# Attention scores on small TensorE pieces with VectorE turns, and a new order of first loads and weight conversions

## The chip, the cores and the metric

The kernel runs on one core of a Trainium2 chip. The metric is the device time of one execution in microseconds (us); the time of a kernel is the median of its runs. In the profile, PE is TensorE's products, PEld its weight loads, DVE is VectorE, ACT ScalarE, POOL GpSimd, and SP the engine that issues most loads. POOL's spans are rough, and PE's ends are modelled.

## What is computed

A memory attention over 8 batches of 8 heads with 576 positions and 32 memory slots feeds a gated layer (512 to 1536 to 512) and an ELU layer (512 to 2048 to 512). The weights come as float64; q and k are scaled by 200.

```python
a = softmax(phi, axis=2)                       # over 576 positions
k_m = einsum('bhsm,bhsd->bhmd', a, k)
v_m = einsum('bhsm,bhsd->bhmd', a, v)
attn = softmax(q @ k_m.T / sqrt(64))           # over 32 slots
x = (attn @ v_m) rearranged to 4608 x 512
x = (silu(x @ w_gate) * (x @ w_val)) @ w_out   # the first layer
g = x @ w_in
out = where(g > 0, g, exp(min(g, 0)) - 1) @ w_out2
```

## The kernel before

Every weight goes through `load_w` (L86 to L112): SP loads 128x512 pairs of words, ScalarE scales the high word (L100), VectorE makes four passes (L101, L102, L104, L105), and then GpSimd adds the two parts (L111, for gate and value weights) or, for the others, ScalarE rounds to the high part (L107) and GpSimd makes the low part in two operations (L108, L109). This is called a conversion below. A product of the layers is three TensorE instructions of 288 columns: high by high, high by low, low by high.

Stage one runs eight loops, one for each batch `b`. Batch b + 2 goes through `front_tasks`: the exponents of phi (L216 to L223), their transposes `a_T` (L234), the products with k and v `kv_mm` (L247: 40 instructions of 128 rows, 32 columns of weights and 128 moving columns; the page shows two records for each fp32 instruction), the scaling by VectorE `kv_out` (L255) and the transposes `kv_T` (L263). Batch b + 1 goes through `back_tasks`: `score` (L282, with q as the weights, positions on the partitions, the 32 slots of two heads side by side), softmax over groups of 32 (L286 to L297), and the transposes back with the split into high and low parts, `attn_T` (L307 to L311). `vw_tasks` multiplies v_m into the gate and value weights (L139, eight instructions of 64 rows by 32 columns with 512 moving columns; L143 and L144 split the result into VW). Between these stand the loop's own products: for both halves of 288 positions and UA = 4 units, `gate1` (pg), `val1` (pv, then h at L183, hh at L162 and hl at L164), and the output product `down1` (pd) of the half before, which goes to DRAM. The function `tick` takes the next few pieces from the list `todo` after each product; `spread` says over how many ticks the list lasts. Conversions stand in the same list: the pairs 2 to 5 of gate and value weights, one pair (four conversions) in each of the loops 1 to 4, and `w_out` for the units 4 to 6 in loop 6 and 7 to 11 in loop 7. Loop 7 also makes the VW of pairs 2 and 3 for batch 0.

Stage two runs the units 4 to 11 of all batches, with the attention reloaded (`load2`) and part sums from DRAM; stage three is the second layer. Conversions of its weights (`more_w2`) stand in both.

The order of the instructions on each engine is fixed when the program is built, by a scheduler that follows its own model of times; it goes by the order of the code, except that `together` keeps a group of products in one piece and `issue_after` binds one instruction behind another. On the chip each engine goes through its own list in order. The loads of SP stand in one such list too; a load waits for its buffer (two for raw weights, `wr_p`; six each for kv and q).

## Time and profile before

| what | value |
|---|---|
| median of three runs | 1632.61 us (1631.53 to 1634.37) |
| the profiled execution | 1629.19 us, its span 1627.4 us |
| mean granted clock of TensorE | 0.982 |
| busy PE / PEld | 1577.3 us (97%) / 1358.8 us (83%) |
| busy DVE / ACT / POOL | 962.4 (59%) / 659.3 (41%) / 169.4 us (10%) |
| moved by DMA | 136.34 MB |

Stage one ends at 388.6 us. A busy share is a mean over stages that differ; the rows by stretches further below show one for each loop. PE is counted busy while any product is in flight, so 100% doesn't say that it streams at its peak.

### The profile page before, as it was taken

The page shows a single profiled execution, that of the slowest core. Times are in us where ns is not written, and L with a number is a line of the kernel's source. Part 1 is how long each engine was busy: PE and PEld are TensorE (multiplying, and loading weights), DVE is VectorE, ACT ScalarE, POOL GpSimd, SP SyncE. Part 2 cuts the span into 40 slices and gives each one's busy share as a digit, 9 for nine tenths or more (in the row PEclk, how much of TensorE's full clock was granted, in tenths as well). Part 3 has the DMA queues.
Part 4 walks back from the last instruction along what each step waited for, and adds up shares of the span by engine and source line. Part 5 has one row for each costly group of instructions (what it writes and reads, how often), then busy time and mean ns, then how long its engine had stood idle before and what let it go on. Part 6 is the DMA issues. An engine that isn't in the chain of part 4 may idle for free.

```text
span 1627.4 us, 24651 instructions
## 1 busy us (share of the span) xinstructions
PE 1577.3 (97%) x9968; PEld 1358.8 (83%) x9968; DVE 962.4 (59%) x1718; ACT 659.3 (41%) x1281; POOL 169.4 (10%) x135
## 2 busy tenths in 40 slices
PE   6699999999999999999999999999999999999998
PEld 4588888888999999999987788888888888888887
DVE  5778777665444544443799755555555555555554
ACT  3455444454333333333455443434343434343333
POOL 1211111132011010100244200000000000000000
PEclk7699999999999999999999999999999999999999
DMA  8877443243222322221242010101010101010000
GB/s 300 272 251 251 166 140 133 76 167 108 73 94 82 101 74 83 85 87 45 87 149 91 34 33 0 52 1 52 1 52 1 52 0 53 1 52 0 26 1 26
DMA packets 65906, 136.34 MB, mean 84 GB/s; under 512 B 6912, under 2 KB 38656, under 8 KB 63744
## 3 DMA queue, kind: packets, MB, share of 16 engines
...
q14 instruction: 36, 0.29, 0.1%
...
## 4 chain that ended last, share of the span: by engine, by line
PE 80%; DVE 9%; DMA 7%; ACT 2%; issue 1%; SPq 0%; ACTq 0%; DVEq 0%
PE pu L534 7%; PE pu L535 7%; PE pu L533 7%; PE acc L559 7%; PE acc L560 7%; PE acc L561 7%; PE acc L156 4%; PE acc L158 4%; PE acc L157 4%; PE pg L151 3%; PE pv L151 3%; PE pvw L139 3%; PE pg L153 3%; PE pg L152 3%; PE pv L152 2%; PE pv L153 2%
## 5 line engine op out<-in xcount | busy, mean ns | idle before, releaser
L561 PE MATMUL acc<-whi,hl 128*128 128x512 f32 x576 | 222.5, 391 | 2.8 <-DVE hl L164 2.8
L559 PE MATMUL acc<-whi,hh 128*128 128x512 f32 x576 | 224.3, 389 | 0.1
L560 PE MATMUL acc<-wlo,hh 128*128 128x512 f32 x576 | 224.1, 389 | 0.0
L533 PE MATMUL pu<-x1s,whi 128*128 128x512 f32 x576 | 224.1, 389 | 0.0
L534 PE MATMUL pu<-x1s,whi 128*128 128x512 f32 x576 | 224.1, 389 | 0.0
L535 PE MATMUL pu<-x1s,wlo 128*128 128x512 f32 x576 | 224.1, 389 | 0.0
L548 DVE SCALAR_TENSOR_TENSOR g<-e,g 128x512 f32<-128x512 f32 x144 | 103.7, 720 | 159.2 <-ACT g L547 159.2
L162 ACT ACTIVATE hh<-g 128x512 fp32r<-128x512 f32 x144 | 91.0, 632 | 212.8 <-DVE g L549 209.4
L183 DVE SCALAR_TENSOR_TENSOR h<-s,pv 128x288 f32<-128x288 f32 x192 | 86.5, 450 | 146.5 <-PE pv L153 132.5
L546 ACT ACTIVATE e<-g 128x512 f32<-128x512 f32 x144 | 90.8, 631 | 202.8 <-DVE g L545 202.8
L164 DVE TENSOR_TENSOR hl<-g,hh 128x512 fp32r<-128x512 f32 x144 | 101.1, 702 | 88.5 <-ACT hh L162 88.4
L156 PE MATMUL acc<-hh,whi 128*128 128x288 f32 x512 | 151.3, 296 | 0.1
L157 PE MATMUL acc<-hh,wlo 128*128 128x288 f32 x512 | 150.5, 294 | 0.0
L158 PE MATMUL acc<-hl,whi 128*128 128x288 f32 x512 | 149.5, 295 | 0.0
L162 ACT ACTIVATE hh<-h 128x288 fp32r<-128x288 f32 x192 | 85.0, 443 | 153.1 <-DVE h L183 152.6
L164 DVE TENSOR_TENSOR hl<-h,hh 128x288 fp32r<-128x288 f32 x192 | 94.5, 492 | 65.0 <-ACT hh L162 65.0
L561 PEld LDWEIGHTS acc<-whi,hl 128*128 128x128 f32 x576 | 108.0, 188 | 28.5 <-DVE hl L164 6.2
L559 PEld LDWEIGHTS acc<-whi,hh 128*128 128x128 f32 x576 | 108.2, 188 | 22.7 <-ACT hh L162 0.5
L534 PEld LDWEIGHTS pu<-x1s,whi 128*128 128x128 f32 x576 | 108.3, 188 | 22.4
L560 PEld LDWEIGHTS acc<-wlo,hh 128*128 128x128 f32 x576 | 108.0, 188 | 22.4
L533 PEld LDWEIGHTS pu<-x1s,whi 128*128 128x128 f32 x576 | 108.1, 188 | 22.3
L535 PEld LDWEIGHTS pu<-x1s,wlo 128*128 128x128 f32 x576 | 108.1, 188 | 22.3
...
## 6 DMA issues: line engine op xcount, KB each, us to landing
...
```

The lines of the kernel that those rows point to most:

```text
L156: mm(ps, lhsT=w[0][:, ms], rhs=hs[0], start=start, stop=False)
L157: mm(ps, lhsT=w[1][:, ms], rhs=hs[0], start=False, stop=False)
L158: mm(ps, lhsT=w[0][:, ms], rhs=hs[1], start=False, stop=stop)
L162: act(out=hh, in_=h, func=AF.Copy)
L164: tt(out=hl, in0=h, in1=hh.bitcast(F32), op=ALU.subtract)
L533: mm(ps, lhsT=wh[:, k, :], rhs=xh, start=k == 0, stop=False)
L534: mm(ps, lhsT=wh[:, k, :], rhs=xl, start=False, stop=False)
L535: mm(ps, lhsT=wl[:, k, :], rhs=xh, start=False, stop=k == KD - 1)
L548: stt(out=g, in0=e, scalar=1.0, in1=g, op0=ALU.add, op1=ALU.mult)
L559: mm(accs[c], lhsT=hs[0][:, cs], rhs=wh, start=u == 0, stop=False)
L560: mm(accs[c], lhsT=hs[0][:, cs], rhs=wl_, start=False, stop=False)
L561: mm(accs[c], lhsT=hs[1][:, cs], rhs=wh, start=False, stop=u == NU2 - 1)
```

## The change

The scores are computed by slot: kT holds the 64x32 pieces of a head as weights, and 288 positions of q move through them. Eight such instructions (L280 of the new kernel) lie side by side on TensorE and fill two PSUM tiles of 128x288, with the slots of four heads on the partitions. VectorE turns each tile in blocks of 32x32 out of PSUM (L285), so that the 32 slots lie along a row; the softmax runs over one tile of 128x576 for each half; a third turn from SBUF to SBUF (L305) brings it back, and ScalarE (L307) and VectorE (L308) split it. The 20 score products and 10 transposes back of a batch, and GpSimd's zeros in kT, go. q comes in two loads instead of five. The last 64 positions of k and v lie on 128 partitions (64 for each group of heads), so `a_T` has nine transposes instead of ten; `kv_mm` runs the columns outside and the two groups inside.

The first loads come in the order phi and kv of batch 0, gate and value weights of pair 0, q of batch 0, pair 1, then phi and kv of batch 1; `front_tasks(1)` and the first four `w_out` conversions move into loop 0, with a spread of 18. The pairs 2 and 3 are converted over the loops 1 to 4, two conversions in each, and the pairs 4 and 5 in loop 7. There are four buffers for raw weights; other pools change their counts, so that 19 conversions of the second layer stand ahead of stage three instead of 20. The old bodies of `score`, `norm` and `attn_T` are above and left out here.

```diff
-NWA = 32
+NWA = 24
 NWB = 16
-NWE = 8
-NWC = 8
-NKV = 6
-NQ = 6
+NWE = 14
+NWC = 10
+NKV = 5
+NQ = 3
...
-    wr_p = ctx.enter_context(tc.tile_pool(name="wr", bufs=2))
+    wr_p = ctx.enter_context(tc.tile_pool(name="wr", bufs=4))
...
         def load_kv(self, c):
-            n = chunk(c)
-            t = self.kvr[c] = fr_p.tile([128, 2, 512], F32, tag="kvr", name="kvr", bufs=NKV)
-            nc.sync.dma_start(out=t[:n], in_=kv[self.b, 128 * c:128 * c + n])
-        def load_q(self, c):
-            n = chunk(c)
-            t = self.qr[c] = bk_p.tile([128, 512], F32, tag="qr", name="qr", bufs=NQ)
-            nc.sync.dma_start(out=t[:, :4 * n], in_=qT[self.b, :, 512 * c:512 * c + 4 * n])
+            t = self.kvr[c] = fr_p.tile([128, 1024 if c < 4 else 512], F32, tag="kvr" if c < 4 else "kv4",
+                                        name="kvr", bufs=NKV if c < 4 else 2)
+            nc.sync.dma_start(out=t, in_=kv[self.b, 128 * c:128 * c + 128] if c < 4 else kv4[self.b])
+        def load_q(self, hf):
+            t = self.qr[hf] = bk_p.tile([128, 4, HS], F32, tag="qr", name="qr", bufs=NQ)
+            nc.sync.dma_start(out=t, in_=qT[self.b, hf].rearrange("p (j s) -> p j s", j=4))
...
         def a_T(self, c0):
             if c0 == 0:
...
+                self.a = fr_p.tile([128, 9, 128], F32, tag="a", name="a")
+            ps = ps_fr.tile([128, 4, 128], F32, tag="at", name="ps_aT")
+            ph = self.ph.rearrange("p g s -> p (g s)")
+            if c0 == 4:
+                nc.tensor.transpose(out=ps[:, 0], in_=ph[:, 512:640], identity=ident)
+                act(out=self.a[:, 8], in_=ps[:, 0], func=AF.Copy)
+                return
+            for i in range(2):
                 for g in range(2):
...
+                    s0 = 128 * (c0 + i) + 640 * g
+                    nc.tensor.transpose(out=ps[:, 2 * i + g], in_=ph[:, s0:s0 + 128], identity=ident)
+            act(out=self.a[:, 2 * c0:2 * c0 + 4], in_=ps, func=AF.Copy)
...
             def head(c, g, j):
-                n = chunk(c)
-                t = self.kvr[c].rearrange("p t (j g d) -> p t g j d", j=4, g=2)
-                o = 128 * g + 32 * j
-                return mm(self.kvp[g][32 * j:32 * j + 32], lhsT=self.a[:n, c, o:o + 32], rhs=t[:n, :, g, j, :],
-                          start=start and c == cs[0], stop=stop and c == cs[-1])
-            together([lambda c=c, g=g, j=j: head(c, g, j) for c in cs for g in (1, 0) for j in range(4)])
+                col = slice(32 * j, 32 * j + 32)
+                if c < 4:
+                    a = self.a[:, 2 * c + g, col]
+                    t = self.kvr[c].rearrange("p (t j g d) -> p g j t d", t=2, j=4, g=2)[:, g, j]
+                else:
+                    r = slice(64 * g, 64 * g + 64)
+                    a, t = self.a[r, 8, col], self.kvr[c][r].rearrange("p (t j d) -> p j t d", t=2, j=4)[:, j]
+                return mm(self.kvp[g][col], lhsT=a, rhs=t, start=start and c == cs[0], stop=stop and c == cs[-1])
+            together([lambda c=c, g=g, j=j: head(c, g, j) for c in cs for j in range(4) for g in (1, 0)])
...
         def kv_T(self):
...
+            self.kT = bk_p.tile([128, 4, M], F32, tag="kT", name="kT", bufs=2)
+            act(out=self.kT, in_=ps[:, 0], func=AF.Copy)
...
-            self.kT = bk_p.tile([128, 4, 2, M], F32, tag="kT", name="kT", bufs=2)
+        def score(self, hf):
+            q = self.qr.pop(hf)
+            ps = [ps_at.tile([128, HS], F32, tag="at", name="ps_sc") for _ in range(2)]
+            def head(j, g):
+                r = slice(64 * g, 64 * g + 64)
+                return mm(ps[g][32 * j:32 * j + 32], lhsT=self.kT[r, j, :], rhs=q[r, j, :], start=True, stop=True)
+            together([lambda j=j, g=g: head(j, g) for j in range(4) for g in (1, 0)])
+            t = self.sc = bk_p.tile([128, 2, HS], F32, tag="sc", name="sc", bufs=2)
             for g in range(2):
-                r, o = slice(64 * g, 64 * g + 64), slice(64 - 64 * g, 128 - 64 * g)
-                nc.gpsimd.memset(self.kT[o, :, g, :], 0.0)
-                act(out=self.kT[r, :, g, :], in_=ps[r, 0], func=AF.Copy)
...
+                nc.vector.transpose(out=t[:, g], in_=ps[g])
+            sc = t.rearrange("p g (b m) -> p (g b) m", m=M)
+            mx = bk_p.tile([128, 2 * HS // M, 1], F32, tag="mx", name="mx", bufs=2)
+            nc.vector.tensor_reduce(out=mx, in_=sc, op=ALU.max, axis=AX.X)
+            tt(out=sc, in0=sc, in1=mx.to_broadcast([128, 2 * HS // M, M]), op=ALU.subtract)
             act(out=sc, in_=sc, func=AF.Exp, scale=1.0 / float(D) ** 0.5)
...
+        def norm(self, hf):
+            sc = self.sc.rearrange("p g (b m) -> p (g b) m", m=M)
+            sm = bk_p.tile([128, 2 * HS // M, 1], F32, tag="smx", name="smx", bufs=2)
             nc.vector.tensor_reduce(out=sm, in_=sc, op=ALU.add, axis=AX.X)
             nc.vector.tensor_scalar_add(out=sm, in0=sm, scalar1=1e-9)
             nc.vector.reciprocal(out=sm, in_=sm)
...
+            tt(out=sc, in0=sc, in1=sm.to_broadcast([128, 2 * HS // M, M]), op=ALU.mult)
+        def attn(self, hf):
+            if hf == 0:
                 self.at = av_p.tile([128, 2, 2, S], F32R, tag="at", name="at")
...
+            t = bk_p.tile([128, 2, HS], F32, tag="ex", name="ex")
+            nc.vector.transpose(out=t.rearrange("p g s -> p (g s)"), in_=self.sc.rearrange("p g s -> p (g s)"))
+            hi, lo = (self.at[:, i, :, HS * hf:HS * hf + HS] for i in range(2))
+            act(out=hi, in_=t, func=AF.Copy)
+            tt(out=lo, in0=t, in1=hi.bitcast(F32), op=ALU.subtract)
...
     def front_tasks(b):
-        z, nxt = Bs[b], Bs[b + 1] if b + 1 < B else None
+        z, nxt = Bs[b], Bs[b + 1] if 0 < b < B - 1 else None
...
     def back_tasks(b):
-        z, nxt = Bs[b], Bs[b + 1] if b + 1 < B else None
-        yield lambda: (z.score(0, 2), nxt and [nxt.load_q(c) for c in (0, 1)])
-        yield lambda: (z.score(2, 4), nxt and [nxt.load_q(c) for c in (2, 3)])
-        yield lambda: (z.score(4, 5), nxt and nxt.load_q(4), 0 < b < B - 2 and Bs[b + 2].phi())
-        yield lambda: z.norm(0, 2)
-        yield lambda: (z.attn_T(0, 2), setattr(z, 'mark1', z.mark))
-        yield lambda: (z.norm(2, 4), z.norm(4, 5))
-        yield lambda: (z.attn_T(2, 5), z.store_at())
+        z, nxt = Bs[b], Bs[b + 1] if 0 < b < B - 1 else None
+        yield lambda: z.score(0)
+        yield lambda: (z.norm(0), nxt and nxt.load_q(0))
+        yield lambda: (z.attn(0))
+        yield lambda: (z.score(1), 0 < b < B - 2 and Bs[b + 2].phi())
+        yield lambda: (z.norm(1), nxt and nxt.load_q(1))
+        yield lambda: (z.attn(1), z.store_at())
...
-    Bs[0].load_phi()
-    for c in range(NCH):
-        Bs[0].load_kv(c)
-    for c in range(NCH):
-        Bs[0].load_q(c)
+    def load(z):
+        z.load_phi()
+        for c in range(NCH):
+            z.load_kv(c)
+    def load_q(z):
+        for c in range(2):
+            z.load_q(c)
+    load(Bs[0])
     Bs[0].phi()
     run(front_tasks(0))
     for k in range(KD):
         load_wg(0, k, wa_p)
-    Bs[1].phi()
+    load_q(Bs[0])
     run(back_tasks(0))
     vw(0, 0, G2)
     for k in range(KD):
         load_wg(1, k, wa_p)
-    with ExitStack() as after:
-        for ins in Bs[0].mark1:
-            after.enter_context(tc.issue_after(ins.ins))
-        run(front_tasks(1))
-        Bs[2].phi()
+    load(Bs[1])
     vw(0, 1, G2)
-    for u in range(UA):
-        load_wo(u, wa_p)
...
+    def wg_tasks(p):
+        return [lambda k=k: load_wg(p, k, wa_p) for k in range(KD)]
...
+        if b == 0:
+            wo = [lambda u=u: load_wo(u, wa_p) for u in range(UA)]
+            f1 = [lambda: (Bs[1].phi(), load_q(Bs[1]))] + list(front_tasks(1)) + [lambda: Bs[2].phi()]
+            for i in range(max(len(wo), len(f1))):
+                todo += wo[i:i + 1] + f1[i:i + 1]
         if 1 <= b <= 4:
-            bk += [lambda k=k, p=b + 1: load_wg(p, k, wa_p) for k in range(KD)]
+            bk += [lambda k=k, p=2 + (b - 1) // 2: load_wg(p, k, wa_p) for k in (0, 1) if b % 2] + \
+                [lambda k=k, p=2 + (b - 1) // 2: load_wg(p, k, wa_p) for k in (2, 3) if b % 2 == 0]
...
-            fr += [lambda: load_wo(7, wb_p), lambda: vw(0, 2, V2), lambda: load_wo(8, wb_p),
-                   lambda: load_wo(9, wb_p), lambda: vw(0, 3, V2), lambda: load_wo(10, wb_p),
-                   lambda: load_wo(11, wb_p)]
+            fr += wg_tasks(4) + [lambda: load_wo(7, wb_p), lambda: vw(0, 2, V2), lambda: load_wo(8, wb_p)]
+            fr += wg_tasks(5) + [lambda: load_wo(9, wb_p), lambda: vw(0, 3, V2), lambda: load_wo(10, wb_p),
+                                 lambda: load_wo(11, wb_p)]
...
-        spread = 16 if b < B - 2 else 24
+        spread = 18 if b == 0 else 16 if b < B - 2 else 24
```

On TensorE, from the VW of pair 0 of batch 0 to the first gate product, before (ps_sc is a score, ps_atT a transpose back, ps_aT and ps_kvm the transposes of phi and the kv products, pvw a VW):

```order
L139 MATMUL pvw<-wg,vt 32x512 x8
L263 MATMUL ps_kvT<-ident,kvm 128x128 x2
L234 MATMUL ps_aT<-ident,ph 128x128 x4
L282 MATMUL ps_sc<-kT,qr 128x2x32 x11
L234 MATMUL ps_aT<-ident,ph 128x128 x4
L282 MATMUL ps_sc<-kT,qr 128x2x32 x5
L282 MATMUL ps_sc<-kT,qr 64x2x32 x4
L234 MATMUL ps_aT<-ident,ph 64x128 x2
L247 MATMUL ps_kvm<-kvr,a 32x128 x40
L307 MATMUL ps_atT<-ident,sc 128x128 x4
L139 MATMUL pvw<-wg,vt 32x512 x8
L151 MATMUL pg<-at,vw 128x288
```

and now:

```order
L139 MATMUL pvw<-wg,vt 32x512 x8
L235 MATMUL ps_aT<-ident,ph 128x128 x8
L229 MATMUL ps_aT<-ident,ph 128x128
L251 MATMUL ps_kvm<-kvr,a 32x128 x40
L265 MATMUL ps_kvT<-ident,kvm 128x128 x2
L280 MATMUL ps_sc<-qr,kT 32x288 x8
L235 MATMUL ps_aT<-ident,ph 128x128 x4
L139 MATMUL pvw<-wg,vt 32x512 x8
L151 MATMUL pg<-at,vw 128x288
```

Half of batch 1's scores and all its transposes back are gone from here; the VW of pair 0 stands ahead of batch 1's whole front.

On TensorE in loop 4, a score of the next batch before, between the loop's gate, value and VW products:

```order
L153 MATMUL pg<-at,vw 128x288
L282 MATMUL ps_sc<-kT,qr 128x2x32
L139 MATMUL pvw<-wg,vt 32x512 x4
L282 MATMUL ps_sc<-kT,qr 128x2x32
L282 MATMUL ps_sc<-kT,qr 64x2x32 x3
L139 MATMUL pvw<-wg,vt 32x512 x4
L282 MATMUL ps_sc<-kT,qr 64x2x32
L151 MATMUL pv<-at,vw 128x288
```

and now, between output and gate products:

```order
L157 MATMUL pd<-hh,wlo 128x288
L158 MATMUL pd<-hl,whi 128x288
L280 MATMUL ps_sc<-qr,kT 32x288 x8
L151 MATMUL pg<-at,vw 128x288
L152 MATMUL pg<-at,vw 128x288
```

The score stood in pieces between other products, and stands in one piece of eight.

On VectorE, the rows up to the first h of stage two, before:

```order
L105 SCALAR_TENSOR_TENSOR wc<-wr,wc 128x512
L183 SCALAR_TENSOR_TENSOR h<-s,pv 128x288
L164 TENSOR_TENSOR hl<-h,hh 128x288
L183 SCALAR_TENSOR_TENSOR h<-s,pv 128x288
L164 TENSOR_TENSOR hl<-h,hh 128x288
L144 TENSOR_TENSOR vw<-pvw,vw 128x512 x3
L183 SCALAR_TENSOR_TENSOR h<-s,pv 128x288
L164 TENSOR_TENSOR hl<-h,hh 128x288
```

and now:

```order
L105 SCALAR_TENSOR_TENSOR wc<-wr,wc 128x512
L101 TENSOR_SCALAR wc<-wv 128x512
L102 SCALAR_TENSOR_TENSOR wv<-wv,wc 128x512
L104 TENSOR_SCALAR wc<-wv 128x512
L105 SCALAR_TENSOR_TENSOR wc<-wr,wc 128x512
L144 TENSOR_TENSOR vw<-pvw,vw 128x512
L101 TENSOR_SCALAR wc<-wv 128x512
L102 SCALAR_TENSOR_TENSOR wv<-wv,wc 128x512
L144 TENSOR_TENSOR vw<-pvw,vw 128x512
L104 TENSOR_SCALAR wc<-wv 128x512
L144 TENSOR_TENSOR vw<-pvw,vw 128x512
L183 SCALAR_TENSOR_TENSOR h<-s,pv 128x288
```

The h and hl of loop 7 stood between the last conversion and stage two; now conversions stand there, up to the first h and behind it.

## Rows read from the trace of the kernel before

**Rows 1.** Busy time by stretches: stretch, length, then busy us (instructions) as headed.

```profile
0.00:67.30 67.30, 45.38 (x400) 34.08 (x400) 40.73 (x83) 23.22 (x49) 13.38 (x23) 0.67 0.86 299
67.30:116.70 49.40, 40.37 (x419) 34.60 (x412) 40.21 (x86) 26.90 (x66) 11.26 (x10) 0.90 0.72 238
116.70:161.00 44.30, 43.38 (x461) 38.22 (x459) 35.52 (x77) 23.76 (x59) 5.90 (x6) 1.00 0.76 251
161.00:201.50 40.50, 40.12 (x372) 35.12 (x369) 31.20 (x72) 20.10 (x49) 5.84 (x6) 1.00 0.53 179
201.50:241.70 40.20, 38.06 (x277) 32.46 (x276) 31.28 (x67) 17.86 (x42) 6.08 (x6) 0.96 0.42 141
241.70:280.90 39.20, 36.78 (x276) 31.64 (x275) 31.24 (x67) 17.56 (x40) 5.76 (x4) 1.00 0.41 138
280.90:317.00 36.10, 36.10 (x277) 31.68 (x276) 21.69 (x51) 15.11 (x36) 0.00 (x0) 1.00 0.18 67
317.00:348.80 31.80, 30.48 (x232) 26.91 (x231) 22.92 (x45) 15.84 (x37) 8.57 (x6) 1.00 0.43 146
348.80:388.60 39.80, 37.65 (x299) 32.93 (x297) 22.88 (x41) 21.11 (x46) 14.96 (x10) 1.00 0.49 173
```

Behind PE stand PEld, DVE, ACT and POOL, then PEclk, the DMA share and GB/s.

**Rows 2.** Page, section 4: shares of the chain that ended last.

```profile
PE 80%; DVE 9%; DMA 7%; ACT 2%; issue 1%; SPq 0%; ACTq 0%; DVEq 0%
```

**Rows 3.** Timeline of TensorE in loop 1: start, us, engine, line, operation, names, shapes.

```profile
123.28 1.00 PE L282 MATMUL ps_sc<-kT,qr 128*128 128x64 f32 x8
124.09 0.38 PE L156 MATMUL pd<-hh,whi 128*128 128x288 f32 x1
```

**Rows 4.** Timeline of TensorE in loop 3.

```profile
203.48 0.29 PE L152 MATMUL pv<-at,vw 128*128 128x288 f32 x1
203.61 0.29 PE L153 MATMUL pv<-at,vw 128*128 128x288 f32 x1
203.74 0.58 PE L307 MATMUL ps_atT<-ident,sc 128*128 128x128 f32 x3
204.25 0.40 PE L156 MATMUL pd<-hh,whi 128*128 128x288 f32 x1
```

**Rows 5.** Timeline of TensorE in stage two.

```profile
429.29 1.09 PE L139 MATMUL pvw<-wg,vt 64*32 64x512 f32 x16
430.31 0.40 PE L151 MATMUL pg<-at,vw 128*128 128x288 f32 x1
```

**Rows 6.** Timeline of TensorE in loop 0.

```profile
111.73 2.53 PE L247 MATMUL ps_kvm<-kvr,a 64*32 64x128 f32 x80
114.19 0.40 PE L151 MATMUL pv<-at,vw 128*128 128x288 f32 x1
```

**Rows 7.** VectorE by line and form, 100 to 350 us: busy, mean ns | idle before.

```profile
L183 DVE SCALAR_TENSOR_TENSOR h<-s,pv 128x288 f32<-128x288 f32 x51 | 22.8, 447 | 4.9 <-PE pv L153 2.5
...
L297 DVE TENSOR_TENSOR sc<-sc,smx 128x512 f32<-128x512 f32 x11 | 8.0, 726 | 0.0
...
L287 DVE TENSOR_TENSOR sc<-ps_sc,mx 128x512 f32<-128x512 f32 x10 | 6.8, 679 | 0.0
...
L216 DVE TENSOR_REDUCE nmx<-ph 128x2 f32<-128x1152 f32 x3 | 4.0, 1346 | 4.0 <-DMA ph<-phiT 4.0
```

**Rows 8.** Timeline of VectorE in loop 7.

```profile
356.76 0.42 DVE L101 TENSOR_SCALAR wc<-wv 128x512 int32<-128x512 int32 x1
...
357.83 0.45 DVE L164 TENSOR_TENSOR hl<-h,hh 128x288 fp32r<-128x288 f32 x1
...
359.26 0.45 DVE L183 SCALAR_TENSOR_TENSOR h<-s,pv 128x288 f32<-128x288 f32 x1
359.62 1.15 DVE L101 TENSOR_SCALAR wc<-wv 128x512 int32<-128x512 int32 x1
...
363.82 0.45 DVE L183 SCALAR_TENSOR_TENSOR h<-s,pv 128x288 f32<-128x288 f32 x1
```

**Rows 9.** Timeline of VectorE at the start; in brackets the idle time before.

```profile
15.37 0.61 DVE L255 TENSOR_SCALAR kvm<-ps_kvm,rs 128x128 f32<-128x128 f32 x2 [7.12 <-PE ps_kvm L247]
```

More of the change, by code (lines that the diff above doesn't have):

```diff
@@ L28, with attention_moe_moe @@
 NCH = 5
-NWA = 32
+NWA = 24
 NWB = 16
-NWE = 8
-NWC = 8
-NKV = 6
-NQ = 6
+NWE = 14
+NWC = 10
+NKV = 5
+NQ = 3
 @with_exitstack
-def attention_moe_moe(ctx: ExitStack, tc: tile.TileContext, qT, phiT, kv, w1g, w1o, w2, out):
+def attention_moe_moe(ctx: ExitStack, tc: tile.TileContext, qT, phiT, kv, kv4, w1g, w1o, w2, out):
     nc = tc.nc
@@ L226, in a_T @@
             if c0 == 0:
-                self.a = fr_p.tile([128, NCH, 256], F32, tag="a", name="a")
-            n = chunk(c0)
-            nch = 2 if n == 128 else 1
-            ps = ps_fr.tile([128, 2, 256], F32, tag="at", name="ps_aT")
-            for i in range(nch):
+                self.a = fr_p.tile([128, 9, 128], F32, tag="a", name="a")
[6 more added lines that the diff above has]
+            for i in range(2):
                 for g in range(2):
-                    s0 = 128 * (c0 + i)
-                    nc.tensor.transpose(out=ps[:n, i, 128 * g:128 * g + 128],
-                                        in_=self.ph[:, g, s0:s0 + n], identity=ident)
-            act(out=self.a[:n, c0:c0 + nch], in_=ps[:n, :nch], func=AF.Copy)
+                    s0 = 128 * (c0 + i) + 640 * g
+                    nc.tensor.transpose(out=ps[:, 2 * i + g], in_=ph[:, s0:s0 + 128], identity=ident)
+            act(out=self.a[:, 2 * c0:2 * c0 + 4], in_=ps, func=AF.Copy)
         def kv_mm(self, cs, start, stop):
@@ L512, in attention_moe_moe @@
                     nxt = load3(0)
-                if u % 2 == 1 if b == B - 1 else u == 8 and b < B - 2:
+                if u % 2 == 1 if b == B - 1 else u == 8 and len(w2q) > 8:
                     more_w2(w2q.pop(0))
@@ L593 @@
     gate, val = (inputs[n].reshape(KD, 128, NU1 // 2, 2, 1, 128) for n in ("moe_w_gate", "moe_w_val"))
+    ph = phi.reshape(B, 4, 2, S, M).transpose(0, 2, 1, 4, 3).reshape(B, 2, 128, S)
+    kvn = np.stack([a.transpose(0, 2, 1, 3).reshape(B, S, DM) for a in (k, v)], axis=2)
     arrays = {
[L595 to L597 removed]
+        "qT": qT.reshape(B, 128, 4, 2, HS).transpose(0, 3, 1, 2, 4).reshape(B, 2, 128, 4 * HS),
+        "phiT": np.stack([ph[:, 0], np.roll(ph[:, 1], 64, axis=2)], axis=1),
+        "kv": kvn[:, :512].reshape(B, 512, 1024),
+        "kv4": kvn[:, 512:].reshape(B, 64, 2, 4, 2, D).transpose(0, 4, 1, 2, 3, 5).reshape(B, 128, 512),
         "w1g": np.concatenate([gate, val], axis=4).transpose(2, 0, 1, 3, 4, 5).reshape(NU1 // 2, KD, 128, 512),
```

40 lines of the change are left out of this document (2 added, 38 removed).

## The prediction

> **What bounds the kernel now.** I read the busy time by stretches first, one for the start and one for each of the eight loops of stage one [rows 1], then the shares of the chain that ended last [rows 2]. The chain is 80% TensorE. In the stretches from 116.7 to 388.6 us TensorE is busy 94 to 100% of the time; only the first two, up to 116.7 (the start and loop 0), are otherwise: TensorE 45.4 of 67.3 and 40.4 of 49.4 us, at a granted clock of 0.67 and 0.90, beside DMA shares of 0.86 and 0.72 and VectorE at 40.7 and 40.2 us. The change touches stage one (loops 0 to 7) and the ends of the later stages, so the sum has three parts: A, from the start to the first gate product of batch 1 (116.7 us); B, loops 1 to 6 (232.1 us); C, loop 7 (39.8 us). It is made against the profiled execution: 1629.2 us, span 1627.4; the median of the runs, 1632.6, lies 3.4 above, which I add at the end.
>
> **B: the score on TensorE.** Old: eight records, which are four of the 20 score instructions of a batch (an fp32 instruction leaves two records), hold TensorE from 123.28 to the next start at 124.09 [rows 3], 0.20 us each; with the late second start after a break I take 0.22. A turn of the weights back costs more: three transposes run from 203.74 to 204.25, against a beat of 0.13 for the products around them [rows 4], so 0.17 each. New: eight instructions of 64 rows by 32 columns and 288 moving columns for half a batch. The trace has the same eight tiles in the VW product, with 512 columns: 429.29 to 430.31, 1.02 us for its eight instructions [rows 5]. Scaled by columns this is 0.57, unscaled 1.02; most of it is streaming, so I take 0.8 with the break. From the two orders I counted what stands in loops 1 to 6: before 100 score instructions and 56 transposes back, after 64 score instructions (eight halves), no transposes back, and 40 kv instructions more, since the new order runs them one batch later. So 100 x 0.22 = 22.0 and 56 x 0.17 = 9.5 go, 8 x 0.8 = 6.4 come, and a kv product of 40 instructions costs 2.46 (111.73 to 114.19 [rows 6]), say 2.6 with its break: B is 22.0 + 9.5 - 6.4 - 2.6 = 22.5 us less.
>
> The kv products change too: neighbours now share a column group (j outside, g inside), where four groups took turns. Before, 80 records in 2.46 us are 31 ns each [rows 6]: several tiles run at once, and the second pass of one instruction doesn't hold back the next tile. Whether a whole second instruction on the same tile does, the trace doesn't show. If not, nothing is lost; if only two run together, the four full chunks (four fifths of 2.46, 2.0) take twice as long and the fifth, now on eight tiles, half: +1.7. I take half of that, 0.8, for the four kv products in B: +3.2, ends 0 and +6.8. The Trainium skill (TensorEngine Tiling (Array Packing), Key Properties) says that different tiles load and multiply in parallel; by that rule two neighbours on one tile don't, and the sum would have the full +6.8.
>
> What else the six loops hold stays: they take 232.1 us for some 212 of TensorE work by the counts of the order (0.13 for each product of 288 columns, and the prices here), and I leave the 20 us between (clock dip, VectorE late for a buffer). VectorE doesn't take over: its busy share was 0.60 to 0.80 [rows 1], each of loops 1 to 4 loses two conversions (below), and a batch's new softmax costs 12.0 us against 10.1. That price: 128x288 out of PSUM takes 0.447, 128x512 takes 0.679 (one input in PSUM) or 0.726 (both in SBUF) [rows 7]. No row shows a 32x32 turn; the nearest is the 288-column read, so a turn is 0.45, and the half is 2 turns 0.9, maximum, subtraction and sum of 576 at 0.76 = 2.3, product and low part 0.82 each, the turn back 0.76, small ops 0.4: 6.0. The Trainium skill (Vector Engine (DVE) Microarchitecture Reference, 3.8) states one element per cycle and lane for this turn; no run here shows it, and it is no term of the sum.
>
> **A: the start.** After the change VectorE sets the pace here. Up to the same point its order holds the same 12 conversions, seven softmax halves and sixteen turns (40.5 us by the prices above), where nine old pieces and ten low parts stood (29.3), and one phi maximum (1.35 [rows 7]), its small ops and one kv scaling fewer (about 1): 8.9 more, 8 net of the overlap of neighbouring rows. So 80.9 + 8 = 89 us of work. Its idle time was 35.8: a first stretch until the data are there, of which 7.1 us were one wait for the kv products [rows 9], and waits for late loads. The new order of loads puts the first weight pieces right behind phi and kv: 3.0 MB and then 0.5, at the 299 GB/s of the first stretch [rows 1] 12 us, so 11 us idle remain at the start. For the rest (kv scaling, transposition, score one behind the other; VW of pair 1 waiting for its fourth conversion and for GpSimd) I take 9. A ends at 11 + 89 + 9 = 109 against 116.7: -7.7. With no idle time behind the start 100; with all of the old 125. The queue of SP carries the same bytes, and q in two loads for five; it waits for weight buffers (now four) and for VectorE's store of batch 0 with the kv loads of batches 2 and 3 behind it. I find these loads 10 to 20 us ahead of or level with their products, and charge nothing; if they are late, it is inside the 125.
>
> **C: the pairs converted later.** Loops 1 to 4 lose eight conversions, loop 7 gets them: 13 instead of 5, and twelve and three quarters stand ahead of the first h of stage two. A conversion alone takes 356.76 to 359.26 with one hl of 0.45 in it: 2.05. While GpSimd works, 359.62 to 363.82: 3.75 [rows 8]. Loop 7 keeps GpSimd busy about half of the time, and the eight need one GpSimd op, not two, so 2.7: 13 x 2.7 = 35, eight h and eight hl at 0.4 net 6.4, seven VW remainders 4.6: 46, and 0.5 for the first h: 46.5 against 39.8 now. TensorE, with some 36 us of its own, waits for VectorE: +6.7. Ends: at 2.05 the loop stays at 39.8, at 3.75 it is 60 (+20).
>
> The last conversion that crosses into stage three lies beside its products, where VectorE has been converting anyway: 0 to 2, I take 0.5. Memsets of kT that GpSimd loses, one ScalarE copy and the wider buffers cost and give nothing; no engine waits for them.
>
> **Sum:** -7.7 - 22.5 + 3.2 + 6.7 + 0.5 = -19.8, so 1609.4 for the profiled execution and 1613 for the median.
>
> **Rivals.**
> 1. Everything falls well: kv products unharmed (-3.2), conversions near 2.2 (-6), A ends at 104 (-5). Time 1599. For: VectorE's rows without GpSimd. Against: GpSimd is there.
> 2. Stage one's end and start eat the gain: conversions at 3.5 (57 in loop 7, +10 on the forecast) and A no earlier than now (+8): 1631, no change. For: the held rows [rows 8]. Against: GpSimd's 1.3 to 1.7 us per op can't hold every conversion.
> 3. Slower: a turn on VectorE costs more than a plain pass. Place: A and loops 1 to 4, where VectorE is nearly as long as TensorE. A has 28 column blocks of 288 to turn, each of the four loops 8; with x over 0.45 each, A grows by 28x and the loops by 32x less the 14 us in which VectorE is shorter than TensorE there. It decides at 60x - 14 = 20, x = 0.57, that is 1.0 us a turn. At 1.35, three times a plain pass: 60 x 0.9 - 14 = +40, time 1653. For: no row shows the op. Against: all VectorE rows here go by elements.
> 4. It doesn't do what it says: the eight score tiles run one by one. Then a half takes eight times 0.5 us, 4.0 for 0.8: +26 in B, 1639 and more. Against: the VW rows [rows 5].
>
> **Chances.** Forecast (1604 to 1622) 0.56; rival 1 0.20; rival 2 0.12; rival 3 0.08; rival 4 0.04. A measurement can tell 0.2%, 3.3 us, from no change. Rival 2 spreads about 1631: 0.04 to faster, 0.06 to same, 0.02 to slower. Faster 0.80, same 0.06, slower 0.14. The range reaches from rival 1's lower side, 1597, to rival 2's middle, 1631.
>
> **What would show it.** Score halves of 0.6 to 1.0 us on TensorE; batch 1 starting at 100 to 118; loops 1 to 6 together near 213; loop 7 near 46 with TensorE waiting for h or VW. Wrong if the turn's row is near 1 us, if kv products take 4 us, or if TensorE waits for kv or q loads in loops 0 and 1.

## The result, and the profile after

The changed kernel takes 1610.6 us (median of 4 runs, 1609.44 to 1611.9) against 1632.7 beside it, a ratio of 0.9864 (95% interval 0.9847 to 0.9881). Forecast were 1613, in 1597 to 1631. Its profiled execution took 1609.4 us, span 1607.6. Made against the profiled execution, the sum of the prediction was -19.8; the two profiled spans differ by 19.8 as well. The agreement to the tenth is luck: three of its five terms were off by 3.7 to 4.8 us, and the errors cancel.

The table gives every run of this study by stretch, in us, from the first gate product of a batch to that of the next (last half: the last half of stage two with the first block of stage three). What is left out, 390.0 and 707.6 us of stages two and three, is the same in all, within 0.3. Block 1 is counted from the first run of its products; in dose_18 one product had been moved ahead of that run, to 892.18, and the run starts at 898.93. Not every stretch holds the same work: in before, two_raw, turns_twice, dose_20, pairs_early and early_wr3 one kv product of 40 instructions (about 2.3 us on TensorE) lies in A that lies in B in the others.

| kernel | start and loop 0 (A) | loops 1 to 6 (B) | loop 7 (C) | first half of stage two | last half and block 0 | time |
|---|---|---|---|---|---|---|
| before | 116.7 | 232.1 | 39.8 | 23.5 | 117.7 | 1632.7 |
| forecast | 109 | 212.8 | 46.5 | as before | +0.5 | 1613 |
| changed | 104.2 | 209.6 | 47.4 | 26.0 | 122.8 | 1610.6 |
| order_alone | 101.3 | 229.8 | 47.4 | 24.9 | 122.7 | 1625.7 |
| two_raw (one run) | 114.0 | 213.5 | 46.5 | 25.6 | 124.0 | 1623.0 |
| old_load_order (one run) | 102.4 | 220.0 | 47.4 | 25.5 | 123.4 | 1618.2 |
| old_load_timed | 105.4 | 213.4 | 47.4 | 26.2 | 123.3 | 1613.9 |
| turns_twice (one run) | 105.1 | 215.7 | 47.4 | 25.0 | 122.7 | 1615.5 |
| kv_one_tile (one run) | 118.7 | 232.7 | 47.4 | 25.6 | 122.7 | 1646.5 |
| dose_18 (one run) | 103.9 | 207.7 | 47.4 | 25.5 | 124.3 | 1608.2 |
| dose_20 | 109.1 | 205.8 | 46.6 | 26.1 | 118.8 | 1606.0 |
| combo | 104.9 | 215.9 | 44.8 | 23.5 | 127.9 | 1616.5 |
| pairs_early | 112.4 | 214.2 | 39.8 | 24.2 | 116.0 | 1607.4 |
| early_wr3 | 106.4 | 214.7 | 40.6 | 24.2 | 119.0 | 1604.4 |
| early_wr4 | 101.5 | 213.0 | 40.5 | 23.5 | 122.7 | 1600.7 |

The busy time by stretches of the changed kernel, start and then loops 0 to 7, in the columns of [rows 1]:

```profile
0.00:55.50 55.50, 23.52 (x266) 11.96 (x266) 43.93 (x74) 20.91 (x41) 14.42 (x17) 0.70 0.91 347
55.50:104.20 48.70, 39.41 (x451) 30.05 (x443) 48.15 (x95) 25.75 (x58) 9.13 (x7) 0.92 0.78 285
104.20:144.50 40.30, 39.21 (x441) 33.20 (x440) 31.28 (x67) 22.87 (x54) 2.56 (x2) 1.00 0.74 266
144.50:183.20 38.70, 37.36 (x433) 32.06 (x432) 30.33 (x65) 19.80 (x46) 2.55 (x2) 1.00 0.52 176
183.20:218.20 35.00, 33.51 (x258) 28.63 (x258) 26.97 (x58) 15.82 (x34) 2.55 (x2) 0.90 0.33 115
218.20:251.60 33.40, 31.05 (x259) 26.55 (x258) 27.02 (x58) 15.84 (x34) 2.57 (x2) 1.00 0.29 103
251.60:280.60 29.00, 28.61 (x226) 26.06 (x226) 19.26 (x43) 13.81 (x31) 0.00 (x0) 1.00 0.22 83
280.60:313.80 33.20, 29.70 (x227) 26.13 (x225) 24.96 (x44) 15.75 (x35) 8.61 (x6) 1.00 0.40 140
313.80:361.20 47.40, 38.31 (x298) 32.84 (x296) 45.77 (x69) 23.63 (x50) 21.35 (x15) 0.99 0.62 208
```

In loop 0 VectorE is busy 48.15 of 48.7 us and in loop 7 45.77 of 47.4, where it had 22.88 of 39.8 [rows 1]; TensorE waits for it there. In loops 1 to 4 VectorE's 27 to 31 us stay under TensorE's 31 to 39. The chain that ended last shows the same shift against [rows 2]: VectorE's share goes from 9 to 14%, that of the transfers from 7 to 2%.

```profile
PE 81%; DVE 14%; DMA 2%; issue 2%; ACT 1%; SPq 0%; POOL 0%; ACTq 0%; DVEq 0%; POOLq 0%
```

The products themselves, on TensorE's timeline in loop 1 (start, us, engine, line, operation, names, shapes):

```profile
109.23 2.40 PE L251 MATMUL ps_kvm<-kvr,a 64*32 64x128 f32 x80
111.56 0.40 PE L156 MATMUL pd<-hh,whi 128*128 128x288 f32 x1
...
116.76 0.72 PE L280 MATMUL ps_sc<-qr,kT 64*32 64x288 f32 x16
117.41 0.40 PE L151 MATMUL pg<-at,vw 128*128 128x288 f32 x1
```

A score of half a batch holds TensorE from 116.76 to 117.41, 0.65 us, where 0.8 had been taken. A kv product of 40 instructions takes 2.33, against 2.46 before [rows 6]. The turns on VectorE, up to the first gate product of batch 1 (busy, mean ns | idle before):

```profile
L289 DVE TENSOR_TENSOR sc<-sc,mx 128x576 f32<-128x576 f32 x7 | 6.9, 985 | 0.0
...
L285 DVE STREAM_TRANSPOSE sc<-ps_sc 128x288 f32<-128x288 f32 x14 | 5.9, 452 | 0.0
...
L305 DVE STREAM_TRANSPOSE ex<-sc 128x576 f32<-128x576 f32 x5 | 3.8, 766 | 0.0
```

A turn out of PSUM takes 0.452 us, as the 0.45 of the prediction; the turn of 288 columns more, from SBUF to SBUF, takes 0.314 more (0.766 - 0.452), 1.09 ns a column. The Trainium skill (Vector Engine (DVE) Microarchitecture Reference, 3.8) has one element per cycle and lane for this turn. The trace agrees as far as it goes: in the plain reads of PSUM a column more costs 1.04 ns (0.679 - 0.447 us for 224 columns [rows 7]), and no row of this turn is dearer.

### The profile page after: what moved, and what is told of

Read it like the earlier page. It is cut to its first block, busy times and chain, and to the rows that moved or that the text cites. A ratio compares the mean times of both kernels' runs of the same rounds, so it can differ in the third digit from the quotient of the medians.

```text
span 1607.6 us, 24193 instructions
## 1 busy us (share of the span) xinstructions
PE 1533.4 (95%) x9816; PEld 1311.5 (82%) x9816; DVE 988.0 (61%) x1702; ACT 654.0 (41%) x1249; POOL 166.2 (10%) x119
## 4 chain that ended last, share of the span: by engine, by line
PE 81%; DVE 14%; DMA 2%; issue 2%; ACT 1%; SPq 0%; POOL 0%; ACTq 0%; DVEq 0%; POOLq 0%
PE acc L565 7%; PE acc L564 7%; PE acc L566 7%; PE pu L538 7%; PE pu L539 7%; PE pu L540 7%; PE acc L156 4%; PE acc L157 4%; PE acc L158 4%; PE pg L151 3%; PE pv L151 3%; PE pv L153 3%; PE pg L153 3%; PE pv L152 3%; PE pg L152 3%; PE pvw L139 3%
## 5 line engine op out<-in xcount | busy, mean ns | idle before, releaser
L553 DVE SCALAR_TENSOR_TENSOR g<-e,g 128x512 f32<-128x512 f32 x144 | 107.5, 747 | 157.5 <-ACT g L552 157.5
L550 DVE TENSOR_SCALAR g<-pu 128x512 f32<-128x512 f32 x144 | 99.1, 689 | 55.2 <-PE pu L540 51.8
L151 PE MATMUL pg<-at,vw 128*128 128x288 f32 x384 | 119.4, 311 | 10.4 <-DVE vw L144 6.0
```

What stands on the lines that cost most here:

```text
L151: mm(ps, lhsT=wh, rhs=ah, start=g == 0, stop=False)
```

## The experiments

**One half of the change alone.** order_alone is the kernel before with the buffers of the change, its order of first loads, the front of batch 1 in loop 0, its conversions in loops 1 to 4 and 7, and its w2q; scores, q, phi and kv stay as before:

```diff
-NWA = 32
+NWA = 24
...
-NWE = 8
-NWC = 8
+NWE = 14
+NWC = 10
...
-    wr_p = ctx.enter_context(tc.tile_pool(name="wr", bufs=2))
+    wr_p = ctx.enter_context(tc.tile_pool(name="wr", bufs=4))
...
```

> The kernel before with only the new order of first loads, the moved front of batch 1, the later pairs, four raw buffers and 19 conversions ahead of stage three; scores as before. Theory (VectorE sets the pace of the start, and its idle time goes by the order of loads; scores pay in loops 1 to 6): the start up to batch 1 falls from 116.7 to 100 to 108 us, loops 1 to 6 stay within 3 us of 232, loop 7 is near 47, and the last half of stage two with block 0 of stage three near 123 instead of 117.6; time 1627 to 1637, about that of before. Rival (the gain at the start comes from the new scores): the start stays at 114 to 118, and the time is 1643 to 1650.

It took 1625.7 us, a ratio of 0.9957 (0.9939 to 0.9975). The start fell to 101.3, B stayed within 2.3 of before, and loop 7 and the last half lost what they lose in the changed kernel: the theory held, stretch by stretch, and the time is 1.3 below its range. So the new scores, with the loads of q and kv and the order of the kv products that come with them, are worth 20.2 us in B (229.8 to 209.6) and cost 2.9 in A, where VectorE has 92.1 us of work instead of 79.5.

**What shortened the start.** The changed kernel with the old order of first loads, and with two raw buffers:

```diff
     load(Bs[0])
+    load_q(Bs[0])
     Bs[0].phi()
     run(front_tasks(0))
+    load(Bs[1])
...
-    load_q(Bs[0])
     run(back_tasks(0))
...
-    load(Bs[1])
```

> The changed kernel with the first loads in the old order: q of batch 0 and phi and kv of batch 1 ahead of the first weights, 7.1 MB instead of 3.0; the front of batch 1 stays in loop 0, and there are four raw buffers. Theory (VectorE idles at the start for want of weights): 4.1 MB at 347 GB/s are 12 us, of which VectorE can fill some with batch 0's softmax; start and loop 0 grow from 104.2 to 107 to 114. Rival (the gain of the start is the moved front and the raw buffers, the order of loads is nothing): 103 to 106.

```diff
-    wr_p = ctx.enter_context(tc.tile_pool(name="wr", bufs=4))
+    wr_p = ctx.enter_context(tc.tile_pool(name="wr", bufs=2))
```

> The changed kernel with two buffers for raw weights instead of four, and nothing else. The start of the kernel with the pairs converted early (two buffers) was 112.4 us, that of the changed kernel 104.2, and the order of loads moved it by under 2. Theory now (the raw buffers carry the gain of the start): start and loop 0 take 110 to 114 us, loops 1 to 6 stay at 206 to 212, the time is 1615 to 1620. Rival (the early pairs did it, by another order of the start): 103 to 106, and 1609 to 1612.

The order of the loads moved A by -1.8 us: the rival. Two raw buffers moved it by +9.8. VectorE's waits up to batch 1 (us in total, times, longest), first of the changed kernel, to 104.2 us, then of two_raw, to 114:

```profile
DVE nmx L212 <- DMA ph<-phiT: 4.9, 1, 4.9
DVE wc L101 <- ACT wv L100: 4.4, 1, 4.4
DVE rs L218 <- ACT ph L215: 1.7, 1, 1.7
DVE smx L295 <- ACT sc L290: 0.4, 1, 0.4
```

```profile
DVE wc L101 <- ACT wv L100: 7.2, 3, 4.4
DVE nmx L212 <- DMA ph<-phiT: 6.3, 3, 4.8
DVE rs L218 <- ACT ph L215: 3.7, 3, 1.7
DVE vw L144 <- ACT vw L143: 1.8, 2, 1.6
DVE s L176 <- ACT s L175: 1.2, 2, 0.7
```

The busy time of two_raw's start and loop 0, in the columns of [rows 1]:

```profile
0.00:114.00 114.00, 69.98 (x796) 47.68 (x796) 90.36 (x173) 49.50 (x107) 22.05 (x23) 0.75 0.85 307
```

VectorE has about the same work, 90.4 against 92.1 us, and idles 23.6 instead of 12.1: it waits for scaled weights, for phi, for VW. In the changed kernel the first three of its waits, 11.0 us, lie in the first 13 us. The scheduler also placed rows otherwise for two buffers (two_raw has one kv product more in A), so the 9.8 are those of the buffers together with the order that they bring. That SP's queue stands waiting for raw buffers is not what the trace shows: up to the first gate product these waits (L88 behind L105) are 15.3 us in two_raw and 14.9 in the changed kernel. How two buffers cost the time stays open, and no run moved the front of batch 1 alone. Time and B of two_raw came out 3 and 1.5 us above the expectation.

The old order of loads cost 10.4 us in B, though. Loop 1 took 49.2 us there:

```profile
102.40:151.60 49.20, 47.27 (x453) 37.75 (x453) 34.23 (x73) 21.70 (x50) 2.55 (x2) 0.83 0.62 217
```

The granted clock is 0.83 (0.50 from 126 to 138 us, the lower level of 1.2 GHz), while TensorE is busy 47.27 of the 49.2 us. That could be chance or come from this order, so it was timed:

> The changed kernel with the first loads in the old order, as looked at before, now in rounds. The one look took 1618.2 us, start and loop 0 at 102.4, and the granted clock at 0.50 between 126 and 138 us, where the changed kernel has 1.00; 12 us at half the clock are 6 lost. Theory A (the order of loads is worth nothing and the clock's fall is not of this order): median 1608 to 1612. Theory B (the fall belongs to this order, since TensorE waits there): median 1616 to 1620, with the fall in the trace again.

The median is 1613.9 (1610.57 to 1615.4), between both theories. In the new profile loop 1 takes 41.5 us at a clock of 1.00, and loop 2 has 0.92. The ratio, 0.9892 (0.9868 to 0.9916), overlaps that of the changed kernel: the medians differ by 3.3 us, so the order of loads is worth little or nothing, and whether it brings these falls of the clock stays open.

**VectorE's time.** Every turn out of PSUM twice:

```diff
                 nc.vector.transpose(out=t[:, g], in_=ps[g])
+                nc.vector.transpose(out=t[:, g], in_=ps[g])
```

> The changed kernel with every turn out of PSUM done twice (0.46 us each by the trace of after), 32 rows more on VectorE. Theory (VectorE sets the pace up to batch 1, TensorE behind it): the start and loop 0 grow from 104.2 by 5 to 8 us (16 rows of 0.46, 7.4), loops 1 to 4 by 0 to 3 together. Rival (the start is set by loads or ScalarE): it grows by less than 2.

A grew by 0.9 instead of 5 to 8, the number of the rival; loops 1 to 4 grew by 6.2 (147.3 to 153.5) instead of 0 to 3. Together 7.1 for 14.5 us of rows: the size is that of the theory, the place isn't. In loops 1 to 4 TensorE is busy as long as in the changed kernel (141.3 and 141.1 us) and idles 12.2 us instead of 6.3, all of it behind VectorE by the trace. VectorE didn't become idle in A; its busy time rose by 1.6 only (92.1 to 93.7), though 6.0 us of turns came. One row of a softmax moved behind the boundary, and other rows changed: the mean of the subtraction went from 0.985 to 0.784 us, that of the low part of h from 0.719 to 0.439, that of the low part of the attention from 0.747 up to 1.101. In the changed kernel's A the long rows of the first two are those beside GpSimd: of seven subtractions, five lie beside no GpSimd operation and take 0.74 to 0.75 us, two lie beside one and take 1.53 and 1.64; of seven low parts of h, five take 0.43 to 0.45 and two 1.31 and 1.53. GpSimd and VectorE at 25 us:

```profile
25.60 1.27 POOL L111 TENSOR_TENSOR wg<-wv,wc 128x512 f32<-128x512 f32 x1 [2.95 <-DVE wc L105]
```

```profile
25.44 0.47 DVE L285 STREAM_TRANSPOSE sc<-ps_sc 128x288 f32<-128x288 f32 x1
25.84 1.64 DVE L289 TENSOR_TENSOR sc<-sc,mx 128x576 f32<-128x576 f32 x1
27.40 0.47 DVE L285 STREAM_TRANSPOSE sc<-ps_sc 128x288 f32<-128x288 f32 x1
```

The subtraction that starts at 25.84, with both inputs in SBUF, lasts 1.64 us until after GpSimd's operation ends at 26.87; the turn at 25.44, out of PSUM, overlaps the same operation and isn't longer than the one at 27.40. The Trainium skill (SBUF — State Buffer, Who interferes with whom) says this: a VectorE operation with two SBUF inputs contends with a GpSimd operation that reads SBUF; one with at most one SBUF input, outside VectorE's two-port modes, doesn't. The trace agrees with both: the subtractions above, and the three turns of A that lie beside a GpSimd operation take 0.44 to 0.48 us, like the eleven others. The old subtraction read PSUM [rows 7]; the new one is open to GpSimd, and the prediction priced it at 0.76.

**kv products on one tile.**

```diff
-            together([lambda c=c, g=g, j=j: head(c, g, j) for c in cs for j in range(4) for g in (1, 0)])
+            together([lambda c=c, g=g, j=j: head(c, g, j) for j in range(4) for c in cs for g in (1, 0)])
```

> The changed kernel with the kv products of a batch ordered by column group: the ten instructions of one 32-column group stand one behind the other, then those of the next, so all neighbours lie on one tile. By the beat of 0.13 us for 288 columns a pass of 128 columns streams for 0.058. Theory (different tiles run together, neighbours on one tile don't): 80 passes of 0.058 one behind the other, 4.6 us for a product of 40 instructions instead of 2.33; loops 1 to 6, with four of them, grow by 8 to 10. Rival (what sets the 2.33 is the issue of 80 passes at 29 ns, whatever the tile): 2.3 to 2.6 and no change of the time.

```profile
125.69 8.88 PE L251 MATMUL ps_kvm<-kvr,a 64*32 64x128 f32 x80
134.50 0.40 PE L151 MATMUL pg<-at,vw 128*128 128x288 f32 x1
```

From 125.69 to 134.50 it takes 8.81 us, 110 ns for each of the 80 passes: one behind the other on a tile, and each nearly twice the 0.058 expected. The time grew by 36 us, 23.1 of them in B, where 8 to 10 were expected. In the changed kernel, with two neighbours on a tile and then the next tile, the same 80 passes take 2.33 us, 29 ns each. Four times 29 is 116, about the 110 of one tile: four column groups run side by side, and two neighbours on a tile don't hold the next tile back.

**How many conversions cross into stage three.** 12 as before, or 14 instead of 13 (dose_20 has three raw buffers, to make the room):

```diff
-NWE = 14
-NWC = 10
+NWE = 16
+NWC = 8
...
-    w2q = [wa_p] * 4 + [we_p] * 7 + [wa_p] * 8
+    w2q = [wa_p] * 4 + [we_p] * 8 + [wa_p] * 8
...
-    w2q = [wb_p] * 8 + [wc_p] * 5
+    w2q = [wb_p] * 8 + [wc_p] * 4
```

and for dose_18

```diff
-NWE = 14
-NWC = 10
+NWE = 12
+NWC = 12
...
-    w2q = [wa_p] * 4 + [we_p] * 7 + [wa_p] * 8
+    w2q = [wa_p] * 4 + [we_p] * 6 + [wa_p] * 8
...
-    w2q = [wb_p] * 8 + [wc_p] * 5
+    w2q = [wb_p] * 8 + [wc_p] * 6
```

> The changed kernel with 20 conversions of the second layer ahead of stage three and 12 in it, as before (we 16, wc 8 buffers, three raw buffers instead of four to make the room). Theory (VectorE is full in block 0, so a conversion less there gives its own time): last half of stage two with block 0 of stage three falls from 122.8 to 117 to 119; stage one moves by up to 4 through the raw buffers. Rival (the 5 us come from the other order of instructions there, not from the count): 121 to 124.

> The changed kernel with 18 conversions ahead of stage three and 14 in it (we 12, wc 12 buffers); stage one is the same. Theory (VectorE full in block 0): last half of stage two with block 0 grows from 122.8 to 126 to 129. Rival (not the count): 121 to 124.

The last half and block 0 fell to 118.8 with 12. With 14 they grew by 1.5, less than expected. All kernels here with 13 have 122.7 to 124.0, whether with two raw buffers or four, and all with 12 have 116.0 to 119.0; combo, with 11, is told below. The first half of stage two and this stretch, of the changed kernel and of before:

```profile
361.20:387.20 26.00, 25.96 (x176) 24.45 (x177) 15.26 (x27) 11.27 (x25) 7.63 (x6) 0.89 0.22 68
777.20:900.00 122.80, 114.85 (x579) 96.69 (x577) 108.89 (x162) 59.45 (x104) 54.74 (x36) 0.99 0.27 86
```

```profile
388.60:412.10 23.50, 23.50 (x181) 22.50 (x178) 11.74 (x24) 9.29 (x21) 3.15 (x2) 1.00 0.07 24
802.10:919.70 117.60, 113.56 (x577) 95.52 (x577) 105.12 (x160) 59.44 (x103) 51.22 (x34) 1.00 0.29 94
```

In the second stretch VectorE works 108.9 of 122.8 us, 89%, as it did before (105.1 of 117.6); in the 390.0 us of stage two ahead of it, it works 183.2.

The count isn't all that changes there. These runs also change the `wc` buffers: eight in all kernels with 12 conversions, ten in all with 13 and in combo, twelve in dose_18. The pool `wc` opens at the end of stage two where the pools of the first layer stood, and `t3`, which holds g of stage three, lies behind it. By the sizes in the kernel, with eight buffers `t3` ends 40.0 KB from the start of these pools, and the part sums `p1` of stage two lay at 40.5 to 45.0 KB; with ten, g lies at 40 to 44 KB, on top of them, and its first use has to wait until the last of these sums is stored (`x1d<-p1l`). That wait stands in the changed kernel, on VectorE and then on TensorE:

```profile
814.59 0.69 DVE L550 TENSOR_SCALAR g<-pu 128x512 f32<-128x512 f32 x1 [3.42 <-DMA x1d<-p1l]
```

```profile
819.52 0.50 PE L538 MATMUL pu<-x1s,whi 128*128 128x512 f32 x1 [2.47 <-DVE g L554]
```

```profile
815.00:830.00 15.00, 12.53 (x49) 9.84 (x48) 13.26 (x21) 9.09 (x15) 4.64 (x4) 0.89 0.17 58
```

In dose_20, with eight buffers, the same operation waits for its product alone:

```profile
808.54 0.69 DVE L550 TENSOR_SCALAR g<-pu 128x512 f32<-128x512 f32 x1 [0.67 <-PE pu L540]
```

In the traces of all ten kernels with ten or twelve `wc` buffers VectorE waits 3.4 to 4.1 us for this store, and g starts within 0.1 us of its landing; in the four with eight (before, dose_20, pairs_early, early_wr3) g starts ahead of it. In the changed kernel TensorE's 2.5 us are half of the 5.1, and the clock of 0.89 over the 15 us around it costs by estimate some 1.6 us more (15 x 0.11). What the conversion itself costs there was not run apart from the buffers; from 13 to 14, with the wait in both, it is 1.5 us.

In the first half of stage two TensorE is busy throughout in both, and the 2.5 us more stand at a granted clock of 0.89 instead of 1.00, right behind a loop 7 in which TensorE waited. All kernels with both pairs late have 24.9 to 26.2 there, those with the pairs early and combo 23.5 to 24.2.

**The pairs back in their place, and better versions.**

```diff
-            bk += [lambda k=k, p=2 + (b - 1) // 2: load_wg(p, k, wa_p) for k in (0, 1) if b % 2] + \
-                [lambda k=k, p=2 + (b - 1) // 2: load_wg(p, k, wa_p) for k in (2, 3) if b % 2 == 0]
+            bk += [lambda k=k, p=b + 1: load_wg(p, k, wa_p) for k in range(KD)]
...
-            fr += wg_tasks(4) + [lambda: load_wo(7, wb_p), lambda: vw(0, 2, V2), lambda: load_wo(8, wb_p)]
-            fr += wg_tasks(5) + [lambda: load_wo(9, wb_p), lambda: vw(0, 3, V2), lambda: load_wo(10, wb_p),
-                                 lambda: load_wo(11, wb_p)]
+            fr += [lambda: load_wo(7, wb_p), lambda: vw(0, 2, V2), lambda: load_wo(8, wb_p),
+                   lambda: load_wo(9, wb_p), lambda: vw(0, 3, V2), lambda: load_wo(10, wb_p),
+                   lambda: load_wo(11, wb_p)]
...
```

> The changed kernel with the pairs 2 to 5 converted in loops 1 to 4 again, four conversions in each, and 20 conversions ahead of stage three (wa 32, we 8, wc 8 buffers; two raw buffers, since four don't fit beside them). Theory (the later pairs cost 7.6 us in loop 7, and the conversion more in stage three about 5): loop 7 returns to 40, the first half of stage two to 23.5, last half and block 0 to 118, -15 us; loops 1 to 4 take eight conversions of about 2.7 us beside VectorE shares of 0.77 to 0.81 and grow by 3 to 10; two raw buffers may cost the start up to 6. Time 1598 to 1612. Rival (VectorE has no room in loops 1 to 4, since a product waits for each of its rows): they grow by the whole 21 us, time 1615 to 1622.

Loop 7 returned to 39.8 and the last half to 116.0; B grew by 4.6, A by 8.2, more than the 6 allowed for, and both could come from the two raw buffers, which alone bring 3.9 and 9.8. The theory held in the rest, at 1607.4. So early pairs and more raw buffers should add up. Both versions are pairs_early with smaller buffers elsewhere, here those of early_wr4:

```diff
-NWE = 8
-NWC = 8
+NWE = 6
+NWC = 10
...
-NQ = 3
+NQ = 2
...
-    wr_p = ctx.enter_context(tc.tile_pool(name="wr", bufs=2))
+    wr_p = ctx.enter_context(tc.tile_pool(name="wr", bufs=4))
...
-                                        name="kvr", bufs=NKV if c < 4 else 2)
+                                        name="kvr", bufs=NKV if c < 4 else 1)
...
-            t = self.sc = bk_p.tile([128, 2, HS], F32, tag="sc", name="sc", bufs=2)
+            t = self.sc = bk_p.tile([128, 2, HS], F32, tag="sc", name="sc")
...
```

> The changed kernel with the pairs 2 to 5 in loops 1 to 4 and 20 conversions ahead of stage three (wa 32, we 8, wc 8), three raw buffers and two q buffers to make the room. Theory (terms add: loop 7 -7.6, first half of stage two -2, last half and block 0 -4 to -7, loops 1 to 4 +5, start +1 to +5 by the raw buffer): 1597 to 1603. Rival (VectorE's work only moves, and the start pays the raw buffer in full): 1606 to 1610.

> The changed kernel with the pairs 2 to 5 in loops 1 to 4, four raw buffers, 19 conversions ahead of stage three (wa 32, we 6, wc 10); two q buffers and single buffers for sc and the last kv chunk make the room. Theory: start 103 to 106, loops 1 to 6 212 to 216, loop 7 40, first half of stage two 24, last half and block 0 122 to 123: 1601 to 1605. Rival (the single buffers hold VectorE or the loads up): start and loops 1 to 6 grow by 5 or more, 1607 and above.

early_wr4 takes 1600.7 us (1600.51 to 1603.33), a ratio of 0.9817 (0.9796 to 0.9839), faster than both kernels. Start and loop 0, loops 1 to 6, loop 7:

```profile
0.00:101.50 101.50, 67.01 (x692) 44.83 (x693) 86.54 (x161) 46.34 (x99) 24.38 (x23) 0.75 0.85 314
101.50:314.50 213.00, 202.00 (x1847) 173.23 (x1846) 180.59 (x365) 107.67 (x242) 30.43 (x22) 0.99 0.50 176
314.50:355.00 40.50, 38.37 (x298) 34.34 (x296) 21.73 (x41) 21.46 (x46) 14.48 (x10) 0.96 0.49 169
```

Its stretches came out within 2 us of the expectation; the start is 1.5 better. It has ten `wc` buffers and VectorE's wait of 3.4 us for the store; no run has early pairs, four raw buffers and eight `wc` buffers together. early_wr3 came out 1.4 above its range, with the start at 106.4 and B at 214.7.

combo converts pair 4 in loops 3 to 5 and makes two conversions more of the second layer in the last half of stage two:

```diff
+        if 3 <= b <= 5:
+            fr += wg_tasks(4)[2:] if b == 5 else wg_tasks(4)[b - 3:b - 2]
...
                     more_w2(w2q.pop(0))
+                if b == B - 1 and hf == 1 and u in (8, 10):
+                    more_w2(wb_p)
```

> The changed kernel with pair 4 converted in loops 3 to 5 (one, one and two conversions; wa 28, we 10 buffers), pair 5 in loop 7, four raw buffers, and two more conversions of the second layer made in the last half of stage two, into the buffers that the finished w_out units leave: 21 ahead of stage three, 11 in it. Theory: loop 7 with four conversions fewer falls from 47.4 to 40 to 42, loops 3 to 6 grow by 0 to 4 together, last half and block 0 fall from 122.8 to 116 to 119; the start stays at 104. Time 1594 to 1602. Rival (VectorE's work has no free place and only moves): 1607 to 1611.

The theory failed. Loop 7 fell by 2.6 only, B grew by 6.3, and the last half with block 0 grew by 5.1, at 11 conversions in stage three:

```profile
790.00:800.00 10.00, 10.00 (x78) 10.00 (x77) 10.00 (x14) 4.99 (x10) 5.29 (x4) 1.00 0.85 262
800.00:810.00 10.00, 7.72 (x53) 6.85 (x52) 9.97 (x15) 5.13 (x11) 5.50 (x4) 1.00 0.41 122
810.00:820.00 10.00, 8.61 (x43) 7.31 (x44) 9.30 (x15) 3.27 (x7) 5.80 (x5) 1.00 0.36 126
820.00:830.00 10.00, 5.27 (x21) 4.01 (x20) 4.87 (x9) 5.39 (x8) 0.42 (x1) 0.82 0.24 86
```

From 790 to 820 us VectorE is full, with two conversions more in the same stretch; TensorE falls to 7.7 and 8.6 of 10 us. In the last row it falls to 5.3, but there VectorE isn't full: it waits for the store that the ten `wc` buffers put ahead of g, and TensorE behind it.

```profile
823.45 1.29 DVE L554 TENSOR_SCALAR g<-pu 128x512 f32<-128x512 f32 x2 [4.08 <-DMA x1d<-p1l]
```

```profile
828.36 0.80 PE L542 MATMUL pu<-x1s,whi 128*128 128x512 f32 x1 [4.73 <-DVE g L558]
```

So the count of conversions in stage three doesn't set this stretch: VectorE's load where the conversions stand and the wait for the store both lengthen it here.

## Why the prediction was right, point by point

**B, right in size.** The priced products gave -22.5, and B as a whole measured -22.5, where -19.3 was forecast with the kv term. That the two numbers are the same is partly luck: TensorE's busy time in B fell by 25.5 (224.9 to 199.4 us), and its idle time, which the prediction left as it was, rose by 3.0. The kv term, +3.2 as the middle of 0 and +6.8, was wrong: by the two rows the change is four times -0.13, and the full +6.8, read out of the tiles' running side by side, didn't come either. The prediction said that its trace didn't show whether a second instruction on the same tile holds back the next tile; it doesn't, and only the ten in a row of kv_one_tile run one by one. Besides, B holds a fall of the clock that was not forecast, 0.90 in loop 3; dose_18, with the same order in stage one, has 33.2 us there instead of 35.0 by its own trace.

**A, right in its work, wrong in its cause.** 89 us of VectorE work and 11 us idle at the start were 92.1 and 11.0 (4.9 + 4.4 + 1.7). The 9 us for the rest did not come: VectorE has hardly a gap behind 13 us. The step that failed is the sentence that the order of the loads brings the start its data and that "the wider buffers cost and give nothing". The order is worth little, and two raw buffers instead of four, with the order of instructions that they bring, take back 9.8 of the 12.5 us.

**C, right.** +6.7 forecast, +7.6 measured, by the mechanism named: TensorE is idle 9.1 us of the loop (47.40 - 38.31), and waits 6.9 us of it for the low part of VW on VectorE (3.5 us of that end with the first gate product of stage two).

**The end of stage two, mis-sized.** The last conversion was put at 0 to 2 us, 0.5 taken; last half and block 0 gave +5.1. "VectorE has been converting anyway" spoke against the step, not for it, since VectorE was 89% busy there before. But about half of the +5.1 is a wait that wider buffers bring, so the same sentence on them failed here too: with ten `wc` buffers g lies on the part sums of stage two, and TensorE waits 2.5 us behind their store, besides the lower clock after it. The first half of stage two's +2.5, at the lower clock, was no term at all.

**The rivals.** A dear turn fell by its row, 0.45 us. Score tiles one by one fell by 0.65 us for eight. Rival 1 met two of its three parts, the kv products and A at 104 (104.2), but loop 7 took 47.4 us, not the 40.5 that it would have had. Rival 2 met neither of its two: loop 7 didn't reach 57, and A ended earlier than before. -12.5, -22.5, +7.6, +2.5 and +5.1 make -19.8.
